# Routed attention into a gated FFN on one core: another lead-in, five pieces at other steps, closing products in another order

## The chip, the cores and the metric

The kernel runs on one core of a Trainium2 chip. The metric is the device time of one execution in microseconds (us), compared by medians. Engines: TensorE (PE in the profile, its weight loads PEld), VectorE (DVE), ScalarE (ACT), GpSimd (POOL) and SyncE (SP), which mostly issues DMAs. Each engine works through its own instructions in order and waits at semaphores for the others.

## What is computed

Attention over 4 batches, 8 heads, 768 tokens and a head size of 64, in which a query sees only the keys whose nearest of 16 centroids is its own; the result goes through a feed-forward block with a sigmoid gate (512 to 1536 and back).

```
q_assign = argmax(q_n @ c_n^T)            # per head, 16 centroids, normalised
k_assign = argmax(k_n @ c_n^T)
scores = where(q_assign == k_assign, q @ k^T / sqrt(64), -1e9)
attn_out = softmax(scores) @ v
x = attn_out as 3072 tokens x 512
out = (sigmoid(x @ w_gate) * (x @ w_val)) @ w_out
```

## The kernel before

**Steps.** The work is laid out by hand in 384 steps. A step is one score product of a key chunk (128) against three query chunks (384), line L893, its exponential on ACT (L898), and, two or three steps later, three value products (L916). Batch 0 has steps 0 to 95, batch 1 96 to 191, batch 2 192 to 287, batch 3 288 to 383. A head of a pair p takes 12 steps; of the last pair two times 6. Between the products of a step lies FFN work (gate L530, value L546, output L684 or L821), taken from a queue by a budget of time, and every other piece of work is issued at a step that the table SCHED names. Its numbers are offsets to the step at which the pair is first used: `"b3p1lg0": -32` puts the first head's logits of batch 3, pair 1 (first used at step 312) at step 280. A piece is emitted in program order at its step, so its place decides what stands ahead of it on each engine; no engine reorders.

**A head's pieces.** k and q are split into a high and a low half-precision part (`hi` casts, `lo` subtracts; L1114 and L1121 in the lead-in, L1458 and L1459 later), transposed (`tu` by TensorE in batch 0, L1142, copied out of PSUM by `ev`, L1153 on ACT or L1155 on DVE; later by a DMA issued by SP), multiplied with the centroids (`lg`, L421 or L434), the largest of 16 picked on DVE (`pk`: L449, L460, L462, L469; L1170 and L1178 in the lead-in), the one-hot rows transposed (`ot`, L1202) and placed into rows 64 to 80 of T (`pl`, L1223, L1227), so that the score product brings the mask with it. `vs`, `vu`, `vt` make the sum of v over the tokens: two and one additions on DVE (L330, L336, L337), then one product with ones (L341) and a copy (L346). At the end of a head's av, DVE adds that sum (t, L370), takes the reciprocal (L372), POOL multiplies (xp, L375), and SP transposes xp by DMA into xTb, which the gate products of the FFN read.

**Lead-in.** Before step 0 a list of its own, `"seq"`, gives the order for the first head: `W5` and `N5` are five warm-up products of 512 or of 128 columns (dummies, L984) whose result nobody reads; `hi_1_A_0` is the cast of q (1) on ACT of part 0; k (0) comes in two parts of three chunks; `ca` to `cd` normalise the centroids, transpose them (L301) and split them into cm; `s` lets the planned pieces of a step run. `"l0"` orders the first loads: `c` the centroids, `Sk0` the first part of k on SP, `A..` on ACT, `K` and `Q` the second head's on SP.

**PSUM.** Four banks go round (ring) for scores, gate, value, logits and the v sums; two for attention outputs; two for the FFN's outputs, which a pair of token blocks uses by Strassen-Winograd's seven products, each added on DVE (L768) before its bank is used again.

**Closing.** The last 384 tokens' FFN (L594, L580, L611) works with two pairs a and b of seven products each. Product 7 accumulates in the bank of product 6, and 3 in that of 5, so 6's and 5's additions (into C12 and C22) come first. Product 2 comes last and is cut in two halves for pair b.

Of the kernel before, what the change touches and what calls it, by code (L numbers as in the profile page):

```python
# [94 lines left out]
}  # L95


@with_exitstack
def kernel(
# [12 lines left out]
    PE, ACT, DVE, POOL, SP = nc.tensor, nc.scalar, nc.vector, nc.gpsimd, nc.sync  # L112
    B, H, S, D = q.shape
    NCL = centroids.shape[1]
    DM = out.shape[1]
# [45 lines left out]
    def bank(n=512, dt=FP, name="bank"):  # L161
        return ring.tile([128, n], dt, tag="ring", name=name)
# [14 lines left out]
    WOP = SCHED.get("wop", 2)  # L177
    WON = NFC // WOP
    wo = [wpool.tile([128, WON, DM], HP, name=f"wo{i}") for i in range(WOP)]
    WB = 0  # L180
    warm = wo[0][:, 0, :]
    POOL.memset(warm, 0.0)
    ident = const.tile([128, 128], FP, name="ident")
    identh = const.tile([128, 128], HP, name="identh")
    make_identity(nc, identh)
# [1 line left out]
    ones = const.tile([128, 128], HP, name="ones")  # L187
    ohs = [const.tile([128, NCH, 128], HP, name=f"oh{i}") for i in range(3)]

    DVE.memset(ones, 1.0)  # L190
    DVE.memset(ohs[0], 0.0)
    POOL.memset(ohs[1], 0.0)
    POOL.memset(ohs[2], 0.0)
# [19 lines left out]
    cen = const.tile([128, D], FP, name="cen")  # L213
# [13 lines left out]
        c = slice(0, Q0) if side == "q" else slice(KC, NCH) if part else slice(0, KC)  # L227
        eng.dma_start(out=RAW[side, 0, 0][:, 0, c], in_=view(side, 0, 0)[:, 0, c])

    load_cen = lambda: ACT.dma_start(out=cen, in_=centroids.rearrange("h c d -> (h c) d"))  # L230
    for x in SCHED.get("l0", ["c", "Sk0", "Aq0", "Sk1", "K", "Q"]):
        if x == "c":
            load_cen()
# [29 lines left out]
    HF, HD = NFC // 2, DM // 2  # L263
# [130 lines left out]
    T = {}  # L394
# [102 lines left out]
    def tok(b, t, f):  # L497
        return HB[b, t // 3][:, HF * f : HF * f + HF, bass.ts(t % 3, 128)]

    def store(src, b, c0, n, m=slice(0, DM)):  # L500
        def f():
            SP.dma_start(
                out=out[b * S : (b + 1) * S].rearrange("(p c) m -> p c m", c=NCH)[
                    :, c0 : c0 + n, m
                ],
                in_=src,
            )

        d_ = SCHED.get("sd", 0)
        if d_ > 0 and b < B - 2:  # L510
            at(step_no[0] + d_, f)
        else:
            f()
# [61 lines left out]
    def closing(b, gv, ma, mb):  # L575

        ac, order = [], []
        plus = lambda dst, a, z: DVE.tensor_tensor(dst, a, z, ALU.add)  # L580

        def pair(m, bk):
            st = {}
            lhs = {
                1: lambda: tok(b, m.t1, 0), 2: lambda: tok(b, m.t1, 1), 4: lambda: tok(b, m.t2, 1),
                6: lambda: m.of[2], 5: lambda: m.of[1], 7: lambda: m.of[3], 3: lambda: m.of[4],
            }
            rhs = {1: B11, 2: B21, 3: B22, 4: T4, 5: T1, 6: T2, 7: T3}
            C = lambda i, j: st["ob"][:, i, HD * j : HD * j + HD]

            def mm(o, k, g, n, start, a=0, z=HD):
                w = lhs[k]()
                for c in range(g, g + n):
                    PE.matmul(  # L594
                        out=o, lhsT=w[:, c, :], rhs=rhs[k][:, c, a:z],
                        start=start and c == 0, stop=c == HF - 1, skip_group_check=True,
                    )

            def product(k, g=0, n=HF):
                def f():  # L600
                    z = {1: "a", 4: "d", 6: "x", 7: "x", 5: "y", 3: "y"}[k]
                    if g == 0 and k in (1, 4, 6, 5):
                        if k == 1:
                            st["ob"] = osp.tile([128, 2, DM], FP, name="ob")
                        st[z] = bk(z)
                    o = st[z][:, 0:HD]
                    mm(o, k, g, n, k not in (7, 3))
                    if g + n < HF:
                        return
                    if k == 1:  # L610
                        ACT.activation(C(0, 0), o, AF.Copy)  # L611
                    elif k == 4:
                        plus(C(1, 0), o, C(0, 0))
                    elif k == 6:
                        plus(C(0, 1), o, C(0, 0))
                    elif k == 5:
                        plus(C(1, 1), o, C(0, 0))
                    elif k == 7:
                        plus(C(1, 0), o, C(1, 0))
                        plus(C(1, 1), o, C(1, 1))  # L620
                        store(st["ob"][:, 1:2], b, m.t2, 1)
                    else:
                        plus(C(0, 1), o, C(0, 1))
                        store(st["ob"][:, 0:1, HD:DM], b, m.t1, 1, slice(HD, DM))

                return f

            def last(parts):
                def f():
                    for a, z in parts:  # L630
                        o = bank(z - a, name="o_end")
                        mm(o, 2, 0, HF, True, a, z)
                        plus(st["ob"][:, 0, a:z], o, st["ob"][:, 0, a:z])
                    store(st["ob"][:, 0:1, 0:HD], b, m.t1, 1, slice(0, HD))

                return f

            return product, last

        two = {}  # L640

        def bank_a(z):
            if z in "ad":
                need(*(("wo", i) for i in range(WOP)), *(("wt", i, c) for i in range(4) for c in range(2)))
                two[z] = out_bank()
            return two[{"x": "a", "y": "d"}.get(z, z)]

        pa, la = pair(ma, bank_a)
        pb, lb = pair(mb, lambda z: bank(512, name="o_end"))
        early = [pa(k, g, HF // 2) for k in (1, 4, 6, 5) for g in (0, HF // 2)]  # L650

        def drained(f):
            def g():
                while aside:
                    aside.pop(0)[1]()
                f()

            return g

        early[0] = drained(early[0])  # L660
        atoms = gv[:14]
        for i, x in enumerate(gv[14:]):
            atoms.append(x)
            if i < len(early):
                atoms.append((0.0, early[i]))
        for f in (
            pa(7), pb(1), pb(4), pa(3), pb(6), pb(5), la([(0, HD)]), pb(7), pb(3),
            lb([(0, HD // 2), (HD // 2, HD)]),
        ):
            atoms.append((0.0, f))  # L670
        return atoms
# [280 lines left out]
    def at(i, f):  # L952
        bg.setdefault(max(i, step_no[0] - 0.5), []).append(f)
# [11 lines left out]
    def need(*names):  # L965
        for n in names:
            assert n in done, n
# [5 lines left out]
    def dummies(n, m=512):  # L973
# [3 lines left out]
        for i in range(n):  # L977
            if WB:
                PE.matmul(
# [121 lines left out]
    def first(p, e, parts=1):  # L1101

        h, st = 2 * p + e, {}
# [4 lines left out]
            return (0, NCH) if parts == 1 else ((0, KC), (KC, NCH))[part]  # L1108

        def hi(s, eng=None, part=0):  # L1110
            if s == 0 and part == 0:
                st["hl"] = hlp.tile([128, 12, 128], HP, tag="hl", name="hl")
            a, z = rng(s, part)
            (eng or DVE.tensor_copy)(  # L1114
                st["hl"][:, a:z, 0:64], RAW["kq"[s], 0, p][:, e, a - 6 * s : z - 6 * s]
            )
# [27 lines left out]
        def ev(s, eng=None, part=0):  # L1144
            if SCHED.get(f"hD{h}", 0):
                return
            if s == 0 and part == 0:
                T[0, h] = tp.tile([128, 12, 128], HP, tag="T", name="T")
            a, z = rng(s, part)
            dst = T[0, h][:, a:z, :].rearrange("p c t -> p (c t)")  # L1150
            src = st["ps", s, part][:, 0 : 128 * (z - a)]
            if eng is ACT:
                ACT.copy(dst, src)  # L1153
            else:
                DVE.tensor_copy(dst, src)  # L1155
# [173 lines left out]
    a = P[0, 0, 0]  # L1329
# [79 lines left out]
    for b, p, e in P:  # L1409
        if b + p + e == 0:  # L1410
            continue
        d = P[b, p, e]
# [116 lines left out]
    for b in range(B):  # L1529
        xT = xtp.tile([128, NDC, S], HP, tag="xTb", name="xTb")  # L1530
        key = min(b, 1)
        for i in range(2 if b else NPT):
# [4 lines left out]
            c0, cn = PARTS[i] if b == 0 else (3 * i, 3)  # L1537
            for w in range(1 + (cn > 3)):
                z = cn // (1 + (cn > 3))
# [51 lines left out]
```

## Time and profile before

| | us |
|---|---|
| median of 3 runs | 322.78 |
| lowest and highest | 322.7 and 324.16 |
| the profiled execution | 323.67 |
| its span, from the first to the last instruction | 321.9 |

The profile's page lists the busy time of each engine as a share of the span, the chain of work that ended last (followed back from the end, at each step to what released it), and the costliest groups. The timeline lists instructions by start, duration, engine, line, operation and tile, out<-in, with the number of merged ones (x) and, in brackets, the idle time before them and what ended it. A row of the chain has start, duration and what. A row of the DMA view has the KB of one transfer and the median us from issue to landing. TensorE's products are pipelined: the time from one start to the next is its real pace, and the duration of a row also has the last one's way through the array.

### The profile page before, as it was taken

To read this page: it belongs to the slowest core of one execution; us is meant where nothing else is said; L and a number is where in the kernel's file an instruction comes from. 1 tells how busy PE (TensorE), PEld (TensorE's weight loads), DVE (VectorE), ACT (ScalarE), POOL (GpSimd) and SP (SyncE) were. 2 spreads that over 40 slices of the span, in tenths; PEclk is the share of its full clock that TensorE was granted. 3 is DMA by queue.
4 is the path that set the end of the run, shared out by engine and by line. 5 is a ranking of instruction groups with operands and counts; after the bars stand their busy time and mean duration, and the time that the engine had idled before them with its cause. 6 is when DMAs were issued, how large, how long until landed. Compare 5 with 4: busy or idle time off the path is not lost.

```text
span 321.9 us, 9181 instructions
## 1 busy us (share of the span) xinstructions
PE 314.6 (98%) x3510; PEld 222.4 (69%) x3510; DVE 224.9 (70%) x598; ACT 231.1 (72%) x521; POOL 108.6 (34%) x145
## 2 busy tenths in 40 slices
PE   7999999999999999999999999999999999999996
PEld 5888666766666666666777687566777688667775
DVE  5799656777787677576878587586767356456666
ACT  6688988787888888877867866778877886332320
POOL 6877464154434365433133333414211111000000
PEclk9999999999999999999999999999999999999999
DMA  7999997738876996978884751942503112200103
GB/s 214 374 256 180 244 171 118 210 75 236 238 113 187 163 238 155 223 172 136 108 219 115 217 113 33 314 110 52 111 2 90 40 26 79 77 2 1 65 2 131
DMA packets 77709, 45.16 MB, mean 140 GB/s; under 512 B 56865, under 2 KB 75105, under 8 KB 77665
## 3 DMA queue, kind: packets, MB, share of 16 engines
q1 hardware_dynamic: 73696, 39.73, 49.7%
q0 software_dynamic: 3680, 4.72, 9.0%
q8 instruction: 27, 0.44, 0.6%
q10 hardware_dynamic: 288, 0.13, 0.2%
q14 instruction: 18, 0.14, 0.2%
HBM read 28.34 MB, written 6.29 MB: 108 GB/s over the span
## 4 chain that ended last, share of the span: by engine, by line
PE 89%; DMA 3%; DVE 3%; issue 2%; POOL 1%; SPq 0%; ACT 0%; POOLq 0%; DVEq 0%
PE g L530 19%; PE v L546 19%; PE sc L893 17%; PE av L916 10%; PE o L821 8%; PE o L684 5%; PE lg L434 2%; PE o_end L594 2%; DMA T<-hl 2%; PE lg L421 1%; PE t_ps L1142 1%; PE o L594 1%; DMA xTb<-xp 1%; PE oh_ps L1202 1%; DMA qraw<-in_q_dram 1%
## 5 line engine op out<-in xcount | busy, mean ns | idle before, releaser
L898 ACT ACTIVATE es<-sc 128x384 f16<-128x384 f32 x384 | 174.3, 492 | 40.6 <-PE sc L893 31.9
L893 PE MATMUL sc<-T 128*128 128x384 f16 x384 | 117.8, 326 | 0.4 <-DVE T L1223 0.4
L916 PEld LDWEIGHTS <-es 128*128 128x128 f16 x1152 | 81.3, 98 | 35.9 <-issue 0.8
L916 PE MATMUL av<-va,es 128*128 128x65 f16 x1152 | 97.6, 194 | 0.0
L551 DVE SCALAR_TENSOR_TENSOR hT<-th,v 128x384 f16<-128x384 f32 x96 | 53.0, 553 | 55.6 <-PE av L916 36.0
L530 PE MATMUL g<-xTb,wg 128*128 128x384 f16 x384 | 78.2, 326 | 0.7 <-DMA xTb<-xp 0.5
L546 PE MATMUL v<-xTb,wv 128*128 128x384 f16 x384 | 78.1, 326 | 0.0
L536 ACT ACTIVATE th<-g 128x384 f32<-128x384 f32 x96 | 47.2, 491 | 35.0 <-PE g L530 15.9
L375 POOL TENSOR_TENSOR xp<-t,rec 128x384 f16<-128x384 f32 (+1 forms) x30 | 21.6, 720 | 101.8 <-DVE rec L372 52.3
L530 PEld LDWEIGHTS <-wg 128*128 128x128 f16 x384 | 37.2, 97 | 19.3 <-issue 0.4
L546 PEld LDWEIGHTS <-wv 128*128 128x128 f16 x384 | 37.4, 98 | 18.6
L893 PEld LDWEIGHTS <-T 128*128 128x128 f16 x384 | 37.1, 97 | 0.6 <-DVE T L1223 0.5
L1459 POOL TENSOR_TENSOR hl<-kraw,hl 128x384 f16<-128x384 f32 x22 | 20.2, 920 | 41.1 <-DVE hl L1458 20.5
L1459 POOL TENSOR_TENSOR hl<-qraw,hl 128x384 f16<-128x384 f32 x22 | 20.9, 950 | 9.8 <-DVE hl L1458 9.8
L768 DVE TENSOR_TENSOR ob<-o,ob 128x256 f32<-128x256 f32 (+1 forms) x35 | 17.8, 523 | 7.6 <-PE o L821 6.8
L370 DVE TENSOR_TENSOR t<-av,sv 128x390 f32<-128x390 f32 (+1 forms) x30 | 14.4, 479 | 9.7 <-PE av L916 7.3
L821 PEld LDWEIGHTS <-sum 128*128 128x128 f16 x168 | 16.4, 98 | 5.2 <-issue 0.8
L684 PE MATMUL o<-wo,hT 128*128 128x512 f16 x72 | 19.9, 379 | 0.0
L821 PE MATMUL o<-wo,hT 128*128 128x256 f16 x126 | 19.8, 272 | 0.0
L449 DVE TENSOR_REDUCE lgs<-lg 128x192 f32<-128x384 f32 x23 | 12.7, 551 | 2.8 <-PE lg L434 2.7
L821 PEld LDWEIGHTS <-hT 128*128 128x128 f16 x126 | 12.2, 97 | 3.4
L322 POOL CAST va<-vraw 128x768 f16<-128x768 f32 x15 | 13.0, 869 | 1.9 <-DMA vraw<-in_v_dram 1.9
(158 smaller groups left out, 340.1 us busy)
## 6 DMA issues: line engine op xcount, KB each, us to landing
vraw<-in_v_dram SPq DMA_DIRECT2D x15, 384.0 KB, 4.9
kraw<-in_k_dram SPq DMA_DIRECT2D x14, 384.0 KB, 4.3
qraw<-in_q_dram SPq DMA_DIRECT2D x12, 384.0 KB, 4.2
out_dram<-ob SPq DMA_DIRECT2D x18, 256.0 KB, 2.4
wg<-in_moe_w_gate_dram POOLq DMA_DIRECT2D x2, 768.0 KB, 9.5
wv<-in_moe_w_val_dram POOLq DMA_DIRECT2D x2, 768.0 KB, 10.3
wo<-in_moe_w_out_dram POOLq DMA_DIRECT2D x2, 768.0 KB, 9.3
T<-ohT SPq DMA_DIRECT2D x44, 24.0 KB, 1.9
```

The source lines that it names most:

```text
L375: (eng or POOL).tensor_tensor(x, t[:, 0:nq, 0:64], bcast(rec[:, 0:nq], 64), ALU.mult)
L530: PE.matmul(out=g[:, 0:n], lhsT=wg[fc // WQ][:, dc, fc % WQ, :], rhs=xT[:, dc, t0 : t0 + n], start=(dc == 0), stop=(dc == NDC - 1),)
L536: ACT.activation(th[:, 0:n], g[:, 0:n], AF.Tanh)
L546: PE.matmul(out=w[:, 0:n], lhsT=wv[fc // WQ][:, dc, fc % WQ, :], rhs=xT[:, dc, t0 : t0 + n], start=(dc == 0), stop=(dc == NDC - 1),)
L551: DVE.scalar_tensor_tensor(HB[b, blk][:, fc, 0:n], st[0][:, 0:n], 1.0, w[:, 0:n], ALU.add, ALU.mult)
L684: PE.matmul(out=o, lhsT=HB[b, blk][:, fc, bass.ts(t, 128)], rhs=wo[fc // WON][:, fc % WON, :], start=(fc == 0), stop=(fc == NFC - 1),)
L768: plus = lambda dst, a, z: DVE.tensor_tensor(dst, a, z, ALU.add)
L821: PE.matmul(out=st[z][:, e], lhsT=a[:, c, :], rhs=rhs[:, c, :], start=start and c + e == 0, stop=c == HF - 1, skip_group_check=True,)
L893: PE.matmul(out=sc.rearrange("p (c t) -> p c t", t=128), lhsT=s["k"], rhs=s["q"], start=True, stop=True,)
L898: ACT.activation(es, sc, AF.Exp, scale=SCALE)
L916: PE.matmul(out=av[:, a0 + s["c0"] + i, :], lhsT=s["es"][:, bass.ts(i, 128)], rhs=VA[b, p][:, e, s["j"], :], start=(first and i == 0 and a ...
L1459: POOL.tensor_tensor(hl[:, :, 64:128], r, hl[:, :, 0:64], ALU.subtract)
```

## The change

Four things change.

- Lead-in: the centroids are loaded by SP ahead of k's first part, q's first part by ACT. The order of the first head's pieces, the engines of its casts and subtractions and the warm-up products (7 of 512 columns, then 2 and 8 of 128, in place of 5, 2, 5 and 11) are new. The warm-up operand is the tile of ones, set by DVE, and no longer a part of wo, set by POOL. `c2d` scales the centroids on DVE in place of ACT, `lx` issues the first terms of all logits of the first head ahead of the second terms. `END` is read nowhere.
- Second logits of batch 1, pair 3: from step 139 to 140.
- Batch 3: pair 0's v sums from steps 269, 271 and 290 to 258, 260 and 279; pair 1's first logits and pick from step 273 to 280.
- Closing: the products after the last value product come in another order, and each half of the last product is stored by itself, the second by ACT.

```
-    -40.0, "b1p3lg1": -29, "b1p3pk1": -27.0, ...
+    -40.0, "b1p3lg1": -28, "b1p3pk1": -27.0, ...
...
-    ["c", "Sk0", "Sq0", "Ak1", "K", "Q"], "seq": ["W5", "ca", "hi_0_-_0", "lo_0_D_0",
-    "hi_1_A_0", "cb", "lo_1_D_0", "N2", "tu_0_0", "hi_0_P_1", "lo_0_P_1", "cc", "tu_1_0",
-    "ev_0_-_0", "ev_1_A_0", "cd", "tu_0_1", "ev_0_A_1", "x", "lg_0", "s", "lg_1", "pk_0",
-    "N5", "s", "ot_0", "N11", "pl_0_-_0", "pl_1_-_0", "s", "pk_1", "s"], "lgr": 1, "pn": 1,
+    ["c", "Aq0", "Sk0", "Ak1", "K", "Q"], "seq": ["W7", "ca", "hi_1_-_0", "lo_1_P_0", "hi_0_-_0",
+    "lo_0_P_0", "cb", "hi_0_A_1", "lo_0_P_1", "tu_1_0", "cc", "tu_0_0", "ev_1_A_0", "cd",
+    "ev_0_A_0", "tu_0_1", "ev_0_A_1", "N2", "x", "lg_0", "s", "lg_1", "pk_0", "s", "ot_0",
+    "N8", "pl_0_-_0", "pl_1_-_0", "s", "pk_1", "s"], "lgr": 1, "pn": 1,
...
+    "b3p0vs": -30, "b3p0vu": -28, "b3p0vt": -9, "b3p1lg0": -32, "b3p1pk0": -32, "c2d": 1, "lx": 1, "END": 0,
...
-    WB = 0
-    warm = wo[0][:, 0, :]
-    POOL.memset(warm, 0.0)
+    WB = 1
...
     DVE.memset(ones, 1.0)
+    warm = ones
...
-    load_cen = lambda: ACT.dma_start(out=cen, in_=centroids.rearrange("h c d -> (h c) d"))
+    load_cen = lambda: SP.dma_start(out=cen, in_=centroids.rearrange("h c d -> (h c) d"))
...
-    def store(src, b, c0, n, m=slice(0, DM)):
+    def store(src, b, c0, n, m=slice(0, DM), eng=None):
         def f():
-            SP.dma_start(
+            (eng or SP).dma_start(
...
-                    for a, z in parts:
+                    for a, z, eng in parts:
                         o = bank(z - a, name="o_end")
                         mm(o, 2, 0, HF, True, a, z)
                         plus(st["ob"][:, 0, a:z], o, st["ob"][:, 0, a:z])
-                    store(st["ob"][:, 0:1, 0:HD], b, m.t1, 1, slice(0, HD))
+                        store(st["ob"][:, 0:1, a:z], b, m.t1, 1, slice(a, z), eng)
...
-            pa(7), pb(1), pb(4), pa(3), pb(6), pb(5), la([(0, HD)]), pb(7), pb(3),
-            lb([(0, HD // 2), (HD // 2, HD)]),
+            pa(7), pb(1), pb(4), pb(6), pb(5), pb(7), pa(3), la([(0, HD, SP)]), pb(3),
+            lb([(0, HD // 2, SP), (HD // 2, HD, ACT)]),
...
-            if s == 0 and part == 0:
+            if "hl" not in st:
...
-            if s == 0 and part == 0:
+            if (0, h) not in T:
```

2 rows, old and new, of the table SCHED are left out of this document.

## Prediction

> **What bounds the kernel now.** I read the page first (engine shares, then the chain that ended last), then that chain piece by piece in order of time, and then the timeline around every place where the chain leaves TensorE.
>
> ```profile
> span 321.9 us, 9181 instructions
> PE 314.6 (98%) x3510; PEld 222.4 (69%) x3510; DVE 224.9 (70%) x598; ACT 231.1 (72%) x521; POOL 108.6 (34%) x145
> PE 89%; DMA 3%; DVE 3%; issue 2%; POOL 1%; SPq 0%; ACT 0%; POOLq 0%; DVEq 0%
> ```
>
> TensorE is busy for 98% of the span and makes up 89% of the chain, so the middle of the kernel can only get shorter where TensorE really stands still. Of the change's parts, only four places can therefore count: the lead-in before the stream is dense, one stop near 99 us, a cluster of three stops between 195 and 207 us, and the closing products with the last store.
>
> **Lead-in, first head.** The chain from 0 to 14 us and the timeline of the same stretch (start, duration, what):
>
> ```profile
> 4.75 0.45 PE ct_ps L301
> 5.19 0.69 PE t_ps L1142 x6
> 7.34 0.55 PE wm L984 x5
> 13.05 0.34 PE t_ps L1142 x6
> ...
> 3.43 0.36 DVE L1121 TENSOR_TENSOR hl<-kraw,hl 128x192 f16<-128x192 f32 x1
> 3.71 0.15 DVE L291 TENSOR_SCALAR r<-r 128x1 f32<-128x1 f32 x1
> 4.25 0.55 POOL L1121 TENSOR_TENSOR hl<-kraw,hl 128x192 f16<-128x192 f32 x1
> 4.33 0.68 DVE L1121 TENSOR_TENSOR hl<-qraw,hl 128x192 f16<-128x192 f32 x1 [0.28 <-ACT hl L1114]
> 8.62 0.35 DVE L1227 TENSOR_SCALAR T<-oh_ps 16x384 f16<-16x384 f16 x1
> 9.17 0.53 PE L893 MATMUL sc<-T 128*128 128x384 f16 x1
> 10.11 0.55 POOL L1121 TENSOR_TENSOR hl<-qraw,hl 128x192 f16<-128x192 f32 x1
> 10.97 0.49 PE L1142 MATMUL t_ps<-identh,hl 128*128 128x128 f16 x6
> ...
> kraw<-in_k_dram SPq DMA_DIRECT2D x1, 96.0 KB, 2.3
> kraw<-in_k_dram ACTq DMA_DIRECT2D x1, 96.0 KB, 2.6
> ```
>
> The reader is to see that the first scores start at 9.17, although DVE wrote the last one-hot rows at 8.97 (8.62 + 0.35), and that five warm-up products lie in the chain ahead of the one-hot transposes.
>
> What the change does here. First loads: q becomes first on ACT's queue (as k was on SP's: 2.3 us) and lands at about 3.0; the first k half becomes second, behind the 32 KB of centroids on SP, a place for which the nearest row is the 2.6 us of the k half behind the centroids on ACT: issued at about 1.2 it lands between 3.4 and 3.9; I take 3.6. All of k's and q's splitting subtractions then go to POOL at 0.55 each in place of DVE's 0.36 and 0.68. DVE's reciprocal chain is now queued behind the cast of that k half, ending at about 4.0 where the first step ran at 3.71 before; the scaling of the centroids moves from ACT to DVE, some 0.3 as the other short DVE steps. The centroid transpose so starts at about 4.75 as before, with 4.6 and 5.0 as ends. The transposes for q run before it, those for the two k halves (six, 0.69) behind it, and all three copies out of PSUM are now ACT's, two behind that transpose: about 0.4 later than before the first products with the centroids begin, as DVE made one copy beside ACT. Half of that comes back at once, because all first terms of the products are now issued ahead of the second ones and none waits in between. What then goes away are the five warm-up products (0.55) between the logits and the one-hot transposes. Sum for the first scores: +0.4 - 0.2 - 0.55 is -0.35 if k lands at 3.6, about 0 if it lands at 3.9.
>
> Not all of that reaches the end. The next transposes on TensorE (10.97) read what POOL finishes at 10.66 (10.11 + 0.55), POOL's work hanging on a k load that stays where it was in SP's queue. So at most 0.3 can be kept here; at the other end, with DVE's scaling slowed by POOL as the subtraction at 4.33 was (0.68 against 0.36), the lead-in is 0.3 longer. I take **-0.15**, between them. Taking the memset of the warm-up operand off POOL frees it 0.5 earlier, before its first load is there: nothing.
>
> [...]
>
> **Step 139 to 140.** The second logits of one head wait for a transposing DMA:
>
> ```profile
> 99.40 0.36 PEld L434 LDWEIGHTS <-T 128*128 128x128 f16 x12 [0.25 <-DMA T<-hl]
> 99.72 0.32 PE L893 MATMUL sc<-T 128*128 128x384 f16 x1
> 99.88 0.25 PE L916 MATMUL av<-va,es 128*128 128x65 f16 x3
> ```
>
> One step later, a score product (its slot is 0.16, from 99.72 to 99.88) and three value products (0.09, from there to the next one at 99.97) run ahead of the logits, 0.25 in all, and cover the wait: **-0.25**. If the transposed tile came later by as much, it would be 0.
>
> **Pieces around steps 258 to 290.** TensorE, then DVE, then the xTb transposition and what it releases:
>
> ```profile
> 192.14 0.46 PE L434 MATMUL lg<-cm,T 128*128 128x32 f16 x12
> 194.68 0.49 PE L821 MATMUL o<-vheld,sum 128*128 128x256 f16 x3
> 195.78 0.49 PE L821 MATMUL o<-wo,sum 128*128 128x256 f16 x3 [0.62 <-DVE ob L768]
> 200.48 0.65 PE L530 MATMUL g<-xTb,wg 128*128 128x384 f16 x3
> 201.68 0.32 PE L530 MATMUL g<-xTb,wg 128*128 128x384 f16 x1 [0.54 <-DMA xTb<-xp]
> ...
> 182.75 0.55 DVE L551 SCALAR_TENSOR_TENSOR hT<-th,v 128x384 f16<-128x384 f32 x1 [1.54 <-PE av L916]
> 193.52 0.55 DVE L449 TENSOR_REDUCE lgs<-lg 128x192 f32<-128x384 f32 x1
> 195.05 1.88 DVE L768 TENSOR_TENSOR ob<-o,ob 128x512 f32<-128x512 f32 x3
> 196.85 0.35 DVE L370 TENSOR_TENSOR t<-av,sv 128x195 f32<-128x195 f32 x1
> ...
> 198.06 3.58 DMA xTb<-xp
> ...
> 206.88 0.55 DVE L551 SCALAR_TENSOR_TENSOR hT<-th,v 128x384 f16<-128x384 f32 x1 [0.24 <-PE av L916]
> 207.01 0.32 PE L893 MATMUL sc<-T 128*128 128x384 f16 x1
> 207.49 0.32 PE L530 MATMUL g<-xTb,wg 128*128 128x384 f16 x1
> ```
>
> The three products at 194.68 take 0.33 of the stream, so the next could start at 195.00; it starts at 195.78 (0.78 lost), because DVE reaches the additions that empty its bank only at 195.05. Ahead of them DVE does the sums over v and the logits' pick (193.52 to 195.05). The change moves both away: the sums to steps 258 and 260, beside the 1.54 for which DVE stands idle before 182.75 (the three together are of the size of the 1.5 that the pick takes), the pick to step 280. The first addition then starts when its product is done, near 192.9, and the stop is gone.
>
> What is late next is the chain behind it: the other two additions wait for the product that ends near 194.9 (195.17 less the 0.31 of the logits moved from 192.14), the three together gave 0.63 each, so t starts near 196.1 in place of 196.85, the transposing DMA starts 0.77 earlier and lands near 200.85. TensorE, 0.78 + 0.31 earlier but with the 12 logits products and the one v product put back before it, is at the fourth gate product at 200.25 (200.97 - 0.72) and waits again, 0.65 instead of 0.71. So the first two stops together give 0.78, not 1.49. The whole 1.49 would come if the transposition landed 0.65 sooner than its 3.58; a gain of 0.3 would be left if the pick at step 280, now ahead of DVE's next additions (1.6 us with the sv step), held TensorE: I find those additions about 0.6 before they are needed.
>
> The third stop, 0.32 (207.01 + 0.16 to 207.49), is a gate product waiting for the PSUM bank that DVE frees at 207.43; with the v-sum's bank taken at step 279 and no longer at 290, the four banks come round one later and it gets one that is already free. Together **-1.1**, from -1.8 to -0.3.
>
> **Closing products.** DVE, TensorE and the last stores:
>
> ```profile
> 314.71 0.75 DVE L580 TENSOR_TENSOR ob<-o,ob 128x256 f32<-128x256 f32 x2
> 315.38 0.41 DVE L580 TENSOR_TENSOR ob<-o_end,ob 128x256 f32<-128x256 f32 x1
> 315.71 0.41 DVE L580 TENSOR_TENSOR ob<-o,ob 128x256 f32<-128x256 f32 x1
> ...
> 314.06 0.82 PE L594 MATMUL o<-wo,T 128*128 128x256 f16 x6
> 314.71 0.82 PE L594 MATMUL o_end<-qheld,sum 128*128 128x256 f16 x6
> 316.68 0.82 PE L594 MATMUL o_end<-vheld,sum 128*128 128x256 f16 x6
> ...
> out_dram<-ob SPq DMA_DIRECT2D x4, 128.0 KB, 1.7
> ```
>
> In the new order product 6 starts near 314.06, 5 near 314.72, and 7 would start near 315.38. But 7 accumulates in the bank of 6, so it needs 6's addition, and DVE is behind: two additions of the pair ahead at 314.71, one for product 4 at 315.38, then 6's at 315.71 to 316.12. TensorE stands still from 315.38 to about 316.15. Before, the pair ahead's product 3 and its last half lay there. All six-product groups (0.65 each) are the same in number, so the end is 0.77 later. Against it: the last store is two of 64 KB on two queues instead of one of 128 KB (1.7 us to land, most of it not bytes), some 0.1 less, and product 7's row leaves earlier. **+0.7**, from +0.3 (if the halves land 0.4 sooner) to +0.8.
>
> **Sum.** -0.15 - 0.25 - 1.1 + 0.7 = -0.8. The profiled execution took 323.67 (its span 321.9 and 1.8 around it), so 322.9 for the same execution; it lies 0.89 above the median 322.78 of the runs shown, which gives **322.0**.
>
> **Rivals.**
> 1. TensorE comes to its full pace later. The six transposes cost 0.69 at 5.19 and 0.34 at 13.05, so the pace doubles in between, while the granted clock on the page shows nothing of it. The change takes out eight of the warm-up products after the first logits that keep TensorE streaming; for it, three runs of one kernel lie 1.46 apart (322.7 to 324.16), against it, the first run of warm-up products is longer by two full ones. It decides if the pace changes after 11 us. Price taken from that spread: 322.0 + 1.46 = 323.5, slower than before.
> 2. The closing wait is smaller or the DMA of xTb faster: 0.4 and 0.65 less, so 321.6 or 321.35 for one of them; both, with 0.3 kept in the lead-in, are 1.2 less, 320.8. For it: the row of 3.58 is the exception that a store issued behind it may explain; against it: that store stays behind it.
> 3. The gains are only moved: the pick at step 280 blocks and the lead-in loses 0.3, -0.8 + 0.8 + 0.45 = +0.45, so 323.2. For it DVE's 1.6 us; against it the slack found above.
>
> [...]
>
> **How the numbers follow.** Forecast 0.5, rival 1 0.15, rival 2 0.25, rival 3 0.1. The forecast's own range is 321.1 to 322.9; taking in rivals 2 and 1 it is 320.5 to 323.6, with 0.3 below rival 2 for a pace that comes early. What a measurement can tell from no change is 0.5%, 1.6 us: faster means under 321.17, slower over 324.39. Below 321.17 lie most of rival 2 and the lower edge of the forecast, 0.35; above 324.39 a part of rival 1, with rival 3 on top, 0.09; the rest 0.56.
>
> **What would show it.** Lead-in: first scores near 8.9 to 9.2, and six transposes that end POOL's chain near 10.7. Near 99 us no idle before the logits. The o<-wo,sum products without an idle time, a g product still waiting about 0.6 for xTb, no stop after step 290. In the closing a stop of 0.7 to 0.8 before o_end<-vheld, released by DVE's ob. Wrong would be: no such stop, a wait on DVE near step 281, or transposes of over 100 ns each after 11 us.

## The result, and the profile after

| us | before | after |
|---|---|---|
| median of 20 runs | 323.24 | 324.16 |
| profiled execution | 323.67 | 324.33 |
| its span | 321.9 | 322.6 |

The change makes the kernel 0.26% slower: the ratio is 1.0026, 95% interval 1.0015 to 1.0037, or +0.84 us (+0.48 to +1.20). The ratio leaves out one of the 20 runs after, 328.74, which ran at a lower mean clock (0.988) than the others. The prediction, 322.0 with a range from 320.5 to 323.6, had the wrong sign. The page of the profile after, its span, busy times and shares of the chain:

```profile
span 322.6 us, 9174 instructions
PE 314.2 (97%) x3504; PEld 220.4 (68%) x3504; DVE 225.2 (70%) x597; ACT 231.4 (72%) x521; POOL 108.7 (34%) x145
PE 79%; DVE 6%; DMA 5%; issue 4%; POOL 4%; SPq 1%; ACT 0%; POOLq 0%; DVEq 0%
```

TensorE is as busy as before; what moved is where it stands still. The timeline of TensorE after (start, duration, what, and in brackets the idle time and what ended it), cut to the places of the prediction's steps:

```profile
8.53 0.32 PE L893 MATMUL sc<-T 128*128 128x384 f16 x1 [0.45 <-DVE T L1227]
8.70 0.33 PE L1142 MATMUL t_ps<-identh,hl 128*128 128x128 f16 x3
...
99.31 0.26 PE L916 MATMUL av<-va,es 128*128 128x65 f16 x3
99.70 0.47 PE L434 MATMUL lg<-cm,T 128*128 128x32 f16 x12
...
183.77 0.33 PE L893 MATMUL sc<-T 128*128 128x384 f16 x1
184.16 0.81 PE L546 MATMUL v<-xTb,wv 128*128 128x384 f16 x4
...
194.64 0.49 PE L821 MATMUL o<-vheld,sum 128*128 128x256 f16 x3
194.97 0.49 PE L821 MATMUL o<-wo,sum 128*128 128x256 f16 x3
...
200.03 0.65 PE L530 MATMUL g<-xTb,wg 128*128 128x384 f16 x3
201.59 0.32 PE L530 MATMUL g<-xTb,wg 128*128 128x384 f16 x1 [0.92 <-DMA xTb<-xp]
...
314.27 0.82 PE L594 MATMUL o_end<-kheld,sum 128*128 128x256 f16 x6
315.73 0.82 PE L594 MATMUL o_end<-vheld,sum 128*128 128x256 f16 x6 [0.65 <-DVE ob L580]
```

The reader sees five things. The first scores start 0.64 earlier than the 9.17 of before. The logits near 99 still follow a gap: three value products take 0.09, and the next product starts 0.39 after them. There is a new stop of 0.23 near 184, ahead of a value product of the FFN (0.16 for the score product, 0.39 to the next start). The stop of 0.78 near 195 is gone (0.33 from one start to the next), but the gate product behind it waits 1.08 for xTb in place of 0.71. And the closing stop is there, 0.81 long (six products take 0.65, the next starts after 1.46). All gaps here and below are starts less the pace of what lies between.

In the chain of waits, start, duration and what, the lead-in and the xTb transposition read so:

```profile
3.10 5.93 DMA kraw<-in_k_dram
9.05 0.52 ACT hl L1114
...
11.75 0.88 POOL hl L1121
12.63 0.05 issue
12.68 0.51 PE t_ps L1142 x6
...
197.59 3.96 DMA xTb<-xp
```

The second pair's k, issued at 3.10, lands at 9.03, 0.82 later than before, and POOL's chain behind it ends at 12.63; by step 24 TensorE is where it was.

Last, the waits of SP's queue over the last three microseconds (us in total, times, longest), after and then before:

```profile
SPq L1586 <- DMA out_dram<-ob: 1.4, 1, 1.4
```

```profile
SPq L1586 <- DMA out_dram<-ob: 0.9, 3, 0.4
```

At the program's end SP goes through eight waits for its DMAs' semaphores, in a fixed order, some 0.065 apart. After, the very first of them is the last store's, so seven follow its landing: the last store lands at 321.22 and the span ends at 322.55, 1.33 later. Before, the last store's was the eighth: 320.98 and 321.89, 0.91.

From the two traces the account is: lead-in 0, step 139 0, pieces -0.5, closing stop +0.8, end of the program +0.4 (with the last landing 0.1 sooner after its product), together +0.7 on the span.

### The profile page after: what moved, and what is told of

The parts are those of the page before. It is cut to its first block, busy times and chain, and to the rows that moved or that the text cites. A ratio compares the mean times of both kernels' runs of the same rounds, so it can differ in the third digit from the quotient of the medians.

```text
span 322.6 us, 9174 instructions
## 1 busy us (share of the span) xinstructions
PE 314.2 (97%) x3504; PEld 220.4 (68%) x3504; DVE 225.2 (70%) x597; ACT 231.4 (72%) x521; POOL 108.7 (34%) x145
## 4 chain that ended last, share of the span: by engine, by line
PE 79%; DVE 6%; DMA 5%; issue 4%; POOL 4%; SPq 1%; ACT 0%; POOLq 0%; DVEq 0%
PE v L546 18%; PE g L530 18%; PE sc L893 15%; PE av L916 9%; PE o L821 7%; PE o L684 5%; PE lg L434 2%; DMA kraw<-in_k_dram 2%; DMA T<-hl 2%; DMA xTb<-xp 1%; PE o L594 1%; PE o_end L594 1%; DVE hT L551 1%; POOL xp L388 1%; POOL hl L1121 1%
## 5 line engine op out<-in xcount | busy, mean ns | idle before, releaser
L449 DVE TENSOR_REDUCE lgs<-lg 128x192 f32<-128x384 f32 x23 | 12.7, 551 | 3.1 <-PE lg L434 3.0
```

## The experiments

All times are differences to the kernel before, from the ratio to its runs on the same chip, with the 95% interval in brackets.

### The parts by themselves

*New lead-in alone* ("l0", "seq", the ones as warm-up operand, centroids on SP, c2d, lx; nothing else).

> The kernel before with the new lead-in alone (first loads, engines and order of the first head, warm-up operand), old steps and old closing. Theory (the two traces: what the first head wins is taken back by its second pair's k load landing 0.8 later and POOL's chain behind it): first scores at about 8.5, the score product of step 24 within 0.1 of before, time within 0.15 of the kernel before. Rival 1 (as forecast): -0.15 to -0.3. Rival 2 (the late loads cost more than the trace shows, and are the loss): +0.4 to +0.8.

Measured +0.03 (-0.45 to +0.52). First scores at 8.50, as after, but step 24 is 0.40 earlier than in the profile before. A version with unchanged lead-in (the closing alone) has 0.43. So the traces' own explanation, loads made late by the new order, does not hold by itself: over six profiles with the old lead-in step 24 starts at 23.33 to 23.77, over ten with the new one at 23.27 to 24.86. Two things go with the late ones. The second pair's k, issued at 3.08 to 3.13 in all, lands by 9.03 in thirteen profiles and at 9.20, 9.52 and 9.54 in three; these three have step 24 at 24.86, 24.25 and 24.28. The chain of waits of one of them:

```profile
3.10 6.42 DMA kraw<-in_k_dram
```

And in two (24.41 and 24.86) TensorE's clock is taken back. The windows view of one of them, the later run with the first row stored whole (stretch, its length, busy time and count of TensorE, weight loads, DVE, ACT, POOL, then the granted clock):

```profile
9.00:11.00 2.00, 1.42 (x28) 1.12 (x27) 1.17 (x5) 1.14 (x3) 1.46 (x3) 1.00 1.07 384
11.00:13.00 2.00, 1.76 (x13) 1.33 (x13) 1.58 (x6) 0.98 (x2) 2.00 (x4) 0.53 1.07 391
13.00:15.00 2.00, 2.00 (x37) 1.76 (x36) 1.09 (x3) 1.68 (x3) 1.92 (x4) 0.61 1.08 383
```

of the kernel before:

```profile
9.00:11.00 2.00, 2.00 (x33) 1.83 (x32) 1.43 (x5) 0.86 (x2) 1.92 (x5) 1.00 1.06 373
11.00:13.00 2.00, 1.57 (x26) 1.25 (x23) 1.80 (x8) 0.87 (x2) 1.98 (x3) 1.00 1.07 385
```

and of the closing alone, which has the old lead-in too:

```profile
9.00:11.00 2.00, 1.55 (x28) 1.12 (x27) 1.40 (x7) 0.97 (x4) 1.73 (x4) 1.00 1.05 366
11.00:13.00 2.00, 1.80 (x27) 1.34 (x28) 1.92 (x5) 1.56 (x4) 2.00 (x4) 1.00 1.07 389
```

The 2.00 of the kernel before is no fair comparison, because its products still took twice as long there. The clock records of the trace, from which the granted clock is taken, begin at 10.89 in the profile before, with 1.0 (the view shows 1.00 ahead of that, too); its six transposes took 0.69 at 5.19 and 0.34 at 13.05, so the beginning of the records is read as that of the full pace. With the old lead-in and the full pace since 5.06, in the closing alone, the same stretch has 1.55, close to the 1.42. Nor does the busy time of this stretch decide: two profiles with the new lead-in have 1.36 and 1.25 in it and keep the clock, those of the run with the late stores and of the gate products three steps later. Where the clock is taken back, it is halved for 3.41 (from 11.14, and from 11.77 in the other). Of the timed runs, 16 of 116 with the new lead-in have a mean clock of 0.997 or less, and 8 of 159 with the old; in the changed kernel four such runs take 324.87 on the mean, the others 324.07. So the loss of the clock goes with the new lead-in; that the eight short warm-up products that it lacks are the reason is not shown.

On the good side, the new order makes the first scores 0.23 earlier on the mean (8.57 to 8.80). But that follows the pace and not the order. The clock records begin at 4.31 to 7.04 in nine of the ten profiles with the new lead-in and at 9.82 in one; with the old they begin at 5.06 and 5.74 in two and at 9.64 to 10.89 in four. Where they begin before 6, the first scores come at 8.20 and 8.28 with the old lead-in and at 8.23 to 8.50 with the new (six). The closing alone, with the old lead-in:

```profile
8.20 0.34 PE L893 MATMUL sc<-T 128*128 128x384 f16 x1 [0.21 <-DVE T L1227]
8.37 0.33 PE L1142 MATMUL t_ps<-identh,hl 128*128 128x128 f16 x3
```

At equal pace the new lead-in wins nothing at the first scores, and the times show no gain either.

*The five moved pieces alone.*

```
+"b1p3lg1": -28, "b3p0vs": -30, "b3p0vu": -28, "b3p0vt": -9, "b3p1lg0": -32, "b3p1pk0": -32
```

> The kernel before with the five moved step pieces alone (logits at 139 to 140, sums over v, the logits and pick of the later head). Theory (the two traces): -0.5, with a new stop of 0.23 before a v product near 184 and a wait for xTb of about 1.0. Rival 1 (as forecast): -1.35, no new stop, the wait for xTb at 0.65 and none before the logits near 99. Rival 2 (moves give nothing because DVE's pick at step 280 blocks): 0 or above.

Measured -0.48 (-1.03 to +0.03): the stop of 0.23 near 184 is there again, those of 0.78 and 0.31 are gone, the wait for xTb is 0.69 (about 1.0 was expected), the wait near 99 0.17.

*The closing alone.*

> The kernel before with the new order of the closing products and the last stores split in two alone. Theory (the two traces): a stop of 0.65 to 0.8 before o_end<-vheld, and 0.4 more between the last landing and the end of the span (0.9 before, 1.3 after), as one DMA more shifts which of the final waits is for the last store; together +1.2. Rival 1 (as forecast): +0.7 and no change behind the last landing. Rival 2: the stop is given back by the split stores, +0.2 or less.

Measured +1.52 (+0.97 to +2.07): the stop is 0.81, 1.33 pass behind the last landing, and the half store on ACT's queue lands 2.31 after its issue, where it was 1.63 in the changed kernel.

*All but the closing.*

```
-pa(7), pb(1), pb(4), pb(6), pb(5), pb(7), pa(3), la([(0, HD, SP)]), pb(3),
-lb([(0, HD // 2, SP), (HD // 2, HD, ACT)]),
+pa(7), pb(1), pb(4), pa(3), pb(6), pb(5), la([(0, HD)]), pb(7), pb(3),
+lb([(0, HD // 2), (HD // 2, HD)]),
```

> The changed kernel with the old order of the closing products and the single last store: lead-in and moved steps together. Theory: -0.45 against the kernel before, the sum of the two parts alone (0 and -0.5). Rival 1 (as forecast): -1.5. Rival 2 (the slower time comes out of the lead-in or the steps, not out of the closing): 0 to +0.5.

Measured -0.71 (-1.13 to -0.29). The loss lies in the closing; the rest is a gain, but only half of the -1.5 forecast.

### The closing taken apart

*New order, one last store* (the order of the change, `la([(0, HD)])` and the single store kept).

> The kernel before with the new order of the closing products alone; the last store stays one of 128 KB on SP's queue. Theory (the stop and the end of the program are two losses): the stop of 0.65 to 0.8 before o_end<-vheld is there, the stretch behind the last landing stays at 0.9, the time is +0.8 against the kernel before. Rival 1 (the split stores are the whole loss): 0. Rival 2 (the order lengthens the end too): +1.2 or more, with 1.3 behind the last landing.

Measured +0.81 (+0.32 to +1.26), stop 0.81, 0.91 behind the last landing: the stop and the end of the program are two losses.

*Old order, split last store.*

> The kernel before with the last store split in two of 64 KB on two queues alone, products in the old order. Theory: no stop of TensorE, the last landing about 0.1 earlier, but 1.3 instead of 0.9 behind it, since one DMA more puts the last store's semaphore at the head of SP's list of final waits: +0.3. Rival 1 (as forecast, two smaller stores land sooner and nothing else): -0.1 to -0.4. Rival 2 (the store on ACT's queue lands late, 2.3 after its issue as in the run of the closing alone): +0.8 to +1.0.

Measured +1.49 (+0.90 to +2.04), with both halves landing 2.34 and 2.44 after issue. The longer end of 0.4 does not explain that. The DMA view of the closing-alone kernel from 320 to 321.6 (busy tenths and GB/s in 40 slices of 0.04, then the queues; q10 is ACT's, q1 SP's) shows what does:

```profile
DMA  9997420469996410036899646000000000000000
GB/s 358 410 384 231 154 52 0 154 205 294 333 320 180 116 39 0 0 115 205 256 320 320 180 103 244 0 0 0 0 0 0 0 26 13 26 26 13 0 0 0
...
q10 hardware_dynamic: 144, 0.07, 14.0%
q14 instruction: 1, 0.01, 1.2%
```

and the same stretch of the changed kernel:

```profile
DMA  9999742136999999998310000000000000000000
GB/s 384 410 410 410 231 128 52 26 102 192 282 320 346 359 295 372 333 282 244 103 39 13 0 0 0 0 0 0 0 0 0 0 0 0 0 0 0 0 0 0
...
q10 hardware_dynamic: 144, 0.07, 14.1%
```

In the first, the ACT half store's packets are done by 321.0 but for the last nine or so, which pass alone at 13 to 26 GB/s near 321.4, after a gap of 0.3: one DMA engine's share of sixteen (144 / 16 = 9). In between lies one packet of an instruction queue, which the changed kernel does not have in this stretch (its last comes at 312.05). It starts at 320.99, and its 1.2% of 16 engines and 1.6 us are 0.31: it is over at 321.30, and the nine start at 321.29. In the split-store kernel such a packet runs from 319.72 to 320.50; from 320.50 on nine packets of SP's half follow one by one, and nine of ACT's half behind those. In both kernels with such a packet the last packets trail by 0.5 to 0.7, and the halves that they belong to land 2.31 to 2.44 after issue; the halves of the three kernels without one land after 1.60 to 1.79. That the packet holds back one engine's share is read from these times; no run tests it by itself. The page before lists 27 instruction packets on queue q8, 0.44 MB and so 16 KB each, and 18 on q14, 0.14 MB and so 8 KB each; those that met the last stores are on q14 (0.01 MB each). Why it falls there in the two kernels with the old lead-in and the split store, and not in the three with the new lead-in and the split store, was not tried.

*Changed kernel with as many DMAs as before*, the first pair's row stored whole.

```
-store(st["ob"][:, 0:1, HD:DM], b, m.t1, 1, slice(HD, DM))
+if m is not ma:
+    store(st["ob"][:, 0:1, HD:DM], b, m.t1, 1, slice(HD, DM))
...
-store(st["ob"][:, 0:1, a:z], b, m.t1, 1, slice(a, z), eng)
+z_ = DM if m is ma else z
+store(st["ob"][:, 0:1, a:z_], b, m.t1, 1, slice(a, z_), eng)
```

> The changed kernel, but the first pair's row is stored whole (one store of 256 KB behind its last product) in place of two halves, so that the program has as many DMAs as before; the split last store stays. Theory (which of SP's final waits belongs to the last store is set by the number of DMAs, and costs 0.4): 0.9 behind the last landing instead of 1.3, the stop before o_end<-vheld as in the changed kernel; 0.4 less than the changed kernel, +0.4 against the kernel before. Rival (the longer end comes with the store on ACT's queue): 1.3 behind the last landing, +0.85.

Measured +0.23 (-0.26 to +0.71), with 0.91 behind the last landing. SP's waits at the end now fall on four DMAs, the last store's among the latest, in place of one of 1.4:

```profile
SPq L1588 <- DMA out_dram<-ob: 1.0, 4, 0.3
```

One DMA fewer gives the 0.43 back, with the split store and its ACT queue in place: the count of DMAs sets which wait the last store's is, and so the end; the queue does not.

*Changed kernel with the old order, split store kept.*

> The changed kernel with the old order of the closing products, the last store still split in two on two queues; so lead-in, moved pieces and split store. Theory A (the split costs what the final waits cost, 0.4 less 0.1): no stop before o_end<-vheld, 1.3 behind the last landing, both halves landing 1.6 after their issue, +0.3 above the version with the old closing, -0.4 against the kernel before. Theory B (the half stores land 2.3 to 2.4 after their issue when the two go out within 0.3 of each other, as in the run of the split alone): +1.1 to +1.5 above that version, +0.5 to +0.8 against the kernel before.

Measured -0.03 (-0.68 to +0.61), too wide to choose by time. The trace chooses: no stop, halves landing 1.63 and 1.79 after issue, 1.34 behind the last landing, and no instruction packet in the last eight microseconds. That is theory A's mechanism; B's 2.3 came only where an instruction packet met the stores.

### The pieces taken apart

*Logits and pick alone to step 280.*

```
+"b3p1lg0": -32, "b3p1pk0": -32
```

> The kernel before with one pair of pieces moved alone, the later head's logits and pick from step 273 to 280. Theory (the moved pick alone frees DVE for the additions; the new stop near 184 comes with the sums over v): no stop at 194.9, none near 184, the stop of 0.31 near 207 stays; -0.75 against before at equal xTb transposition. Rival 1 (sums and pick both have to go): a stop of 0.4 or more is left near 194.9, -0.3. Rival 2 (the new stop comes with the pick): 0.23 near 184.

Measured -0.16 (-0.58 to +0.26). The stop near 195 is gone without moving any sum, none is near 184, and the 0.31 near 207 stays, as the theory had it. The time is not: the transposition of xTb took 3.76, and the gate product waits 0.94.

*All but the two sums over v* (new lead-in, old closing, `"b3p0vs"` and `"b3p0vu"` taken out).

> New lead-in and the moved pieces without the two sums over v (which stay at steps 269 and 271; their last piece still moves to 279), old closing. Theory: none of the stops near 184, 195 and 207, so 0.23 below the version with all moved pieces, -0.9 against the kernel before. Rival 1 (the stop near 184 has another cause): as that version, -0.7. Rival 2 (the sums back at their place bring the stop near 195 back): -0.3 or less.

Measured -0.48 (-0.94 to 0.00). None of the three stops is left, so the one near 184 comes with the sums; but the transposition took 4.03 and the wait is 1.15. The trace's semaphores say what changes there: in the five profiles with the sums moved that FFN value product waits for ScalarE's semaphore, last raised 0.04 earlier by the tanh of the gate, and in the other eleven for DVE's, last raised 0.11 earlier by the pick's first step (L449), without a stop.

The wait for xTb, over the profiles whose gate products start at the old step (the run with late stores follows below):

| kernel | transposition | wait | difference |
|---|---|---|---|
| before | 3.58 | 0.71 | 2.87 |
| lead-in alone | 3.97 | 1.11 | 2.86 |
| closing alone | 3.42 | 0.55 | 2.87 |
| new order, one store | 3.16 | 0.29 | 2.87 |
| old order, split store | 3.20 | 0.34 | 2.86 |
| pick alone | 3.76 | 0.94 | 2.82 |
| moved pieces alone | 3.57 | 0.69 | 2.88 |
| after | 3.96 | 1.08 | 2.88 |
| all but the closing | 4.09 | 1.21 | 2.88 |
| all but closing and sums | 4.03 | 1.15 | 2.88 |
| first row stored whole | 4.23 | 1.35 | 2.88 |
| after, old order | 3.76 | 0.88 | 2.88 |

TensorE has 2.87 of work between the issue and the product, whether the pick is moved or not, and the wait is what the transposition takes beyond that. With the pick at its old step it took 3.47 on the mean (five), with the pick moved 3.91 (seven). The two sets overlap (3.16 to 3.97, and 3.57 to 4.23), but on the mean 0.45 of the gain is taken back there.

### The wait for xTb

*Three output stores behind the transposition later* (base of this and the next three: all but closing and sums).

```
-d_ = SCHED.get("sd", 0)
+d_ = SCHED.get("sd", 0) + SCHED.get("sdx", 0) * (270 < step_no[0] < 286)     # "sdx": 8
```

> As the version with all but the sums over v moved and the old closing, but the three output stores that SP issues right behind the xTb transposition come some steps later, behind the next k load. Theory (the transposition took 3.96 to 4.09 where two stores followed it within 1.9, and 3.16 to 3.42 where none did within 2.0): it lands in 3.2 to 3.5, the wait of the gate product falls from 1.15 to 0.3 to 0.6, -0.5 against that version. Rival 1 (its time scatters by itself): any value from 3.2 to 4.1, no change of the time. Rival 2 (any transfer behind it lengthens it, the k load too): about 4.0.

Measured -0.55 (-1.07 to -0.03), where its base has -0.48, the transposition 4.14 with the next k load behind it at 1.25: the theory that the stores lengthen it falls as put; rival 2 or plain scatter is left, and this stays open. For rival 2: the two transpositions with no other DMA issued within 2.0 behind them took 3.16 and 3.42, and thirteen of the fourteen with one at 1.25 took 3.57 to 4.23; against it: the fourteenth took 3.20.

*Gate products one, two and three steps later.*

```
-lag = SCHED.get(f"lag{key}{i}", 8)
+lag = SCHED.get(f"lag{key}{i}" + "_" * (b == 2 and i == 0), SCHED.get(f"lag{key}{i}", 8))
...
+"lag10_": 8.5        # 9.5 for two steps, 10.5 for three; 7.5 before
```

> As the version with all but the sums over v moved and the old closing, but this block's gate products start one step later, so that a score product and three value products stand ahead of the wait for xTb. Theory (what TensorE does ahead of the wait shortens it one for one): the wait is 0.25 shorter at the same landing (the wait is the transposition's time less 3.1 in place of less 2.87), -0.25 against that version, -1.1 against the kernel before. Rival (the shifted products meet another wait later): no change or slower than that version.

Measured -0.84 (-1.32 to -0.36): the transposition took 3.73, the wait 0.59, difference 3.14.

> As the one before with the gate products two steps later. Theory: the wait is 0.5 to 0.6 shorter at the same landing, -0.5 against the version without it. Rival (scores run into ScalarE's exponentials, or the later products meet another wait): no better than one step.

Measured **-1.87 (-2.39 to -1.36)**, 321.53 as median beside 323.09 for the kernel before: transposition 3.70, wait 0.28, difference 3.42. TensorE's timeline around it:

```profile
199.26 0.33 PE L893 MATMUL sc<-T 128*128 128x384 f16 x1
199.43 0.27 PE L916 MATMUL av<-va,es 128*128 128x65 f16 x3
199.53 0.33 PE L893 MATMUL sc<-T 128*128 128x384 f16 x1
199.97 0.83 PE L530 MATMUL g<-xTb,wg 128*128 128x384 f16 x4
200.64 0.25 PE L916 MATMUL av<-va,es 128*128 128x65 f16 x3
```

The four gate products now run in one piece, behind two more steps' score and value products. Of the 0.87 by which the wait is shorter than in the base, 0.33 is a quicker transposition and 0.54 the cover. The profile's span is 1.85 shorter than the base's, but 0.90 of that is there by step 24 already, where the base's k landed at 9.54: not all of the difference is the move's. By the medians the run is 1.56 below the kernel before.

> As the version with the gate products two steps later, but three. Theory (each step covers 0.25 to 0.3 of the wait, and 0.28 is left of it): no wait for xTb, 0.2 to 0.3 below the version with two steps, -2.1 against the kernel before. Rival (at three steps the scores run into ScalarE's exponentials or the products end later in the block): as two steps or slower.

Measured -1.58 (-2.20 to -1.00): no wait for xTb, but a stop of 0.29 ahead of the value products at 200.79, whose weights wait for ScalarE's exponentials (the rival's mechanism), and one of 0.36 ahead of a gate product at 218.37, released by DVE:

```profile
200.34 0.33 PE L893 MATMUL sc<-T 128*128 128x384 f16 x1
200.78 0.14 PEld L916 LDWEIGHTS <-es 128*128 128x128 f16 x3 [0.38 <-ACT es L898]
...
217.85 0.33 PE L893 MATMUL sc<-T 128*128 128x384 f16 x1
218.37 0.81 PE L530 MATMUL g<-xTb,wg 128*128 128x384 f16 x4 [0.20 <-DVE hT L551]
```

Two steps has the lowest time of the versions run, faster than both kernels; the intervals of two and three steps overlap, so which of them is better is open.

## Why the prediction was wrong

**Lead-in, -0.15: about 0 (+0.03, from -0.45 to +0.52).** Several steps held: k's first half landed at 3.46 (3.6 said), the products with the centroids began 0.42 later than before (0.4 said), and POOL's chain behind an unmoved k load ends the lead-in. That the first scores came at 8.53, better than 8.9, was luck: the sum was worked out from rows at half pace (five warm-up products 0.55), and the profile after reached the full pace at 7.04 in place of 10.89. At equal pace the first scores are not earlier. The term was too favourable in its end, too: that load's landing (8.21 to 9.54) covers what the first head wins, and the clock is at times taken back. That is rival 1, half right: the full pace came sooner in most profiles with the new lead-in, not later, but is lost again after 11 us in some runs, for about 0.8. The 0.3 that the range has below rival 2 for a pace that comes early was an estimate, and no run shows it by itself: in the closing alone, with the old lead-in and the full pace from 5.06, step 24 is 0.43 earlier than in the profile before, where that pace came at 10.89; in the profile after it came at 7.04, and step 24 starts at 23.76 beside 23.77. The end of +0.3 rested on one row, the 0.68 beside POOL's subtraction; in the profile after the scaling took 0.54 at 4.13, beside POOL's subtractions from 3.54 to 5.09, and no run shows POOL to be the cause.

**Step 139 to 140, -0.25: right at equal landing, not seen.** The wait is the DMA's time less 4.55 at the old step (4.85, 4.89, 4.91 and 5.02 give 0.30, 0.33, 0.36 and 0.47), and less 4.81 at the new one (4.85, 4.98 and 5.10 give 0.05, 0.17 and 0.30): the 0.25 is there. In the profile after, the DMA took 5.10 in place of 4.85 and hid it; in the other profiles of either version it took 3.3 to 4.44 and nothing waited.

**Pieces, -1.1: -0.86 at equal landings, about half of that in time.** The stops of 0.78 and 0.32 went as forecast. Two things were missed. Moving the sums "to steps 258 and 260, beside the 1.54 for which DVE stands idle before 182.75" looked at DVE's own time; DVE did find the time, and yet a value product of the FFN came to wait 0.23, ending 0.04 after ScalarE's tanh of the gate (184.12). That the sums bring it, the run without them shows, and by the semaphores the product then waits for another engine's release than without them; why the moved sums change that was not tried. And "lands near 200.85" carried 3.58 from one row to another moment; at the new moment the transposition took 0.45 more on the mean. The pick's move alone had freed the stop near 195: the sums were not needed for it.

**Closing stop, +0.77 within the +0.7: right.** It is 0.81 in the four kernels with the new order, and none is there in those with the old. The order alone costs +0.81 (+0.32 to +1.26).

**Split store, -0.1: wrong sign, and the step that failed most.** The halves do land sooner (1.63 after issue to 1.76), but the step priced the store to its landing and not the program's end behind it: one DMA more made the last store's wait the first of SP's eight final ones and no longer the last, +0.43. In two other kernels the halves landed 0.7 to 0.8 later still, behind an instruction packet.

Of the 2.16 between 322.0 and 324.16, 0.46 lies in the base: the median of 3 runs was 322.78, that of 20 is 323.24. For the rest, -0.8 became +0.84 as follows: lead-in and step 139 gave 0 in place of -0.4, the pieces -0.5 to -0.7 in place of -1.1, the closing +1.1 by the traces and +1.55 by the times (-0.71 to +0.84, whose intervals allow both) in place of +0.7. None of the rivals was it: rival 1 came nearest in time and explains some runs, not the median; rival 3's mechanism did not occur (the pick at step 280 held nobody).

## What to carry to other kernels

Price a transfer's landing as a range over several profiles and write the wait behind it as landing less the work ahead of it; that difference repeats to 0.06 while the landing itself scatters by 1. A wait for a transfer can be met by putting work ahead of the instruction that waits: moving the waiter two steps covered 0.54 of the wait at equal landing, while delaying three stores did not shorten the transfer. Before two lead-ins are compared, see at which pace each profile ran: one and the same lead-in had its first scores at 8.20 and at 9.17. At the end of a program count what follows the last landing too, since one DMA more moved the end of the span by 0.43 here, and one fewer gave it back.

## What was not expected of the hardware

- The end of the span follows the last landing by 0.91 or by 1.33, by the place of the last store's semaphore among SP's eight final waits (0.065 each): 0.91 or 0.92 in eleven of twelve kernels with 182 DMAs (1.02 in the other), 1.33 or 1.34 in three with 183, and 1.18 in the fourth, where the half store with the first semaphore landed 0.17 ahead of the other.
- Nine of the 144 packets of a 64 KB store trailed by 0.5 to 0.7 in the two kernels where a packet of an instruction queue passed in the same stretch, and began within 0.01 of its end or of the end of the nine ahead of them.
- With the new lead-in the granted clock was halved for 3.41 us between 11 and 15.2 us in two profiles of ten, although TensorE had been at full pace since 4.31 and 4.94 us. With one and the same lead-in, the old one, the full pace came at 5.06 in one profile and at 10.89 in another.
- The same transfers scatter: the second pair's k, issued at 3.08 to 3.13, lands at 8.21 to 8.79 with the old lead-in (six) and at 8.26 to 9.54 with the new (ten); one transposing DMA near 94.5 takes 3.31 to 5.10, with none between 3.54 and 4.44.
